# Row-tiled paired transposes, a softmax without row max, and shared PSUM banks in a two-block attention kernel

## Chip, cores and metric

One core of a Trainium2 chip. The metric is the device time of one execution in microseconds (us); smaller is better. "PE" is the matmul engine (its weight loads are a row of their own, "PEld"), DVE the vector engine, ACT the activation engine, POOL the general engine, SP the engine that issues the loads. All runs quoted here were classed as fast, and PE's granted clock is given where it matters.

## The reference

Two independent attention blocks A and B, with their outputs side by side. In each there are 16 batch entries, 64 queries, 32 heads, 512 cached keys and a head size of 128, all bf16:

```python
q = (x @ wq).reshape(B, Sq, H, Dh).transpose(0, 2, 1, 3)      # x: 16 x 64 x 640
scores = einsum("bhqd,bhkd->bhqk", q, k_cache) * Dh ** -0.5
p = softmax(scores)
o = einsum("bhqk,bhkd->bhqd", p, v_cache)
out = o.transpose(0, 2, 1, 3).reshape(B, Sq, H * Dh) @ wo      # 16 x 64 x 640
# result: concatenate([out_A, out_B], -1)
```

The caches make up 268 MB of the 295 MB that the core reads, and nothing of them is used twice.

## The kernel before

The kernel is a static software pipeline. Its unit, called a step here, is two heads of two batch entries; there are 256 steps, fully unrolled. Every engine runs its own straight-line list of instructions, and semaphores tie the lists together. K and P are transposed on PE, because in this kernel's matmuls the index that is summed over lies on the partitions of both operands. One `transpose` or `matmul` in this code becomes two PE instructions, a weight load and a matmul.

```python
# PE's order in one step; the numbers are offsets in steps
PE_T = (("TR2", 1), ("QP2", 4), ("KX", 4, 0), ("SM2", 3), ("PV2", 1), ("XT", 0), ("OP2", 0), ("KX", 4, 1))
# ...
def em_KX(e, op):                       # K: 8 transposes of 128x128, twice a step
    # ...
    for t8 in range(8):
        ins = e.transpose(kt_ps[:, t8, :], kn_ring[:, c % NKB, j, hp, t8, :], ident[:, :])
# ...
def em_MX(e, op):                       # row max, on DVE
    ins = e.reduce_max(negmax[:, r:r + 1], s_bank(g % 2), axis=AX.X, negate=True)

def em_EX(e, op):                       # exp and row sum, on ACT
    ins = e.activation(p_ring[:, g % NP, :], s_bank(g % 2), ACTF.Exp, bias=negmax[:, r:r + 1], scale=1.0,
                       accum_out=rowsum[:, r:r + 1])
# ...
def em_TR2(e, op):                      # P: 8 transposes of 128x128 a step
    # ...
    for t in range(4):
        ins = e.transpose(pt_ps[:, sub, t, :], pn_ring[:, g % NPN, t * 128:(t + 1) * 128], ident[:, :])
```

K and V come in loads of 512 KB into rings of five chunks (10 MB together), all issued by SP as soon as a chunk's place is free.

Of the kernel before, what the change touches and what calls it, by code (L numbers as in the profile page):

```python
# [5 lines left out]
BF16 = mybir.dt.bfloat16  # L6
F32 = mybir.dt.float32
ACTF = mybir.ActivationFunctionType
# [3 lines left out]
ENGINES = ("sp", "pe", "act", "dve", "pool")  # L12


class Cfg:
# [4 lines left out]
    NX = 2  # L20
    NXN = 1
    XLEAD = 10
    NQ = 2
    NKT = 2
    NP = 4
    NPN = 3
    NT = 2
    NO = 2
    NR = 8
    PE_T = (("TR2", 1), ("QP2", 4), ("KX", 4, 0), ("SM2", 3), ("PV2", 1), ("XT", 0), ("OP2", 0), ("KX", 4, 1))  # L30
    ACT_T = (("QE2", 4), ("OE2", 1), ("XE", 0), ("EX", 3, 0), ("EX", 3, 1), ("OV", 0), ("ST", -1))
    DVE_T = (("TE2", 1), ("RC2", 2), ("KE", 4, 0), ("MX", 3, 0), ("MX", 3, 1), ("KE", 4, 1), ("OVF", 0))
    POOL_T = (("NM", 0, 0), ("NM", 0, 1))
    TAIL_SPLIT = 2
    SLOT_NS = 3600.0
    DMA_NS = dict(LDK=3100.0, LDV=3100.0, LDWQ=3900.0, LDWO=4300.0, LDX=700.0)


class Op:
# [3 lines left out]
    def __init__(self, eng, kind, idx, reads=(), writes=(), dur=0.0, ts=None, aux=None):  # L43
        self.eng = eng
        self.kind = kind
        self.idx = idx
        self.reads = tuple(reads)
        self.writes = tuple(writes)
        self.sem = None
        self.count = None  # L50
        self.deps = []
        self.waits = []
        self.dur = dur
        self.ts = ts
        self.aux = aux
        self.dma = kind in ("LDK", "LDV", "LDX", "LDWQ", "LDWO", "ST")


STAGES = ("LDW", "LDX", "LDK", "LDV", "KX0", "KE0", "KX1", "KE1", "QP2", "QE2", "SM2", "MX0", "MX1", "EX0", "EX1",
          "RC2", "NM0", "NM1", "TR2", "TE2", "XT", "XE", "PV2", "OE2", "OP2", "OV", "ST")  # L60
STAGE_IDX = {s: i for i, s in enumerate(STAGES)}
SUB_KINDS = ("KX", "KE", "EX", "NM", "MX")


def build_plan(dims, cfg):
# [7 lines left out]
    SPB = HH  # L73
    NPASS = NBLK * NHALF
    NSTEP = NPASS * NBP * SPB
    NMAC = NSTEP // 2
    NCHUNK = NSTEP // G
    NGRP = NPASS * NBP
    HG = HH // G
    MPG = SPB // 2  # L80
    MPP = NBP * MPG
    MPC = G // 2
    KT = dims["KT"]

    def step_info(g):
        grp = g // SPB
        return grp // NBP, grp % NBP, grp, g % SPB

    progs = {e: [] for e in ENGINES}

    def mk(eng, kind, idx, reads, writes, stage, m_ts, sub=0, aux=None, dur=0.0):
        return Op(eng, kind, idx, reads, writes, dur=dur, aux=aux, ts=(m_ts, STAGE_IDX[stage], sub))

    OFF = {}
    for t in cfg.PE_T:
        OFF.setdefault(t[0], t[1])

    def make_op(kind, m, sub):
        g0, g1 = 2 * m, 2 * m + 1
        ps_, bp, grp, h0 = step_info(g0)  # L100
        c = g0 // G
        if kind == "KX":
            return mk("pe", "KX", (m, sub), [("kn", c % cfg.NKB, g0 % G), ("kn", c % cfg.NKB, g1 % G), ("ident",)],
                      [("KTB",)], "KX%d" % sub, m, sub)
        if kind == "KE":
            return mk("dve", "KE", (m, sub), [], [("KTB",), ("ktp", m % cfg.NKT, sub)], "KE%d" % sub, m, sub)
        if kind in ("MX", "EX", "NM"):
            g = 2 * m + sub
            r = g % cfg.NR
            if kind == "MX":  # L110
                return mk("dve", "MX", g, [], [("SB", sub), ("negmax", r)], "MX%d" % sub, m, sub)
            if kind == "EX":
                return mk("act", "EX", g, [("negmax", r)], [("SB", sub), ("p", g % cfg.NP), ("rowsum", r)],
                          "EX%d" % sub, m, sub)
            return mk("pool", "NM", g, [("p", g % cfg.NP), ("recip", r)], [("pn", g % cfg.NPN)], "NM%d" % sub, m, sub)
        r0, r1 = g0 % cfg.NR, g1 % cfg.NR
        if kind in ("XT", "XE"):
            mt = m + cfg.XLEAD
            if mt % MPG != 0 or not (0 <= mt < NMAC):
                return None  # L120
            gq = mt // MPG
            m_ts = mt - cfg.XLEAD + OFF["TR2"]
            if kind == "XT":
                return mk("pe", "XT", gq, [("xn", gq % cfg.NXN), ("ident",)], [("PTB",)], "XT", m_ts, aux=gq)
            return mk("act", "XE", gq, [], [("PTB",), ("xT", gq % cfg.NX)], "XE", m_ts, aux=gq)
        if kind == "QP2":
            return mk("pe", "QP2", m, [("xT", grp % cfg.NX), ("wq", ps_ % 2, h0 // G)], [("QB",)], "QP2", m)
        if kind == "QE2":
            return mk("act", "QE2", m, [], [("QB",), ("qT", m % cfg.NQ)], "QE2", m)
        if kind == "SM2":  # L130
            return mk("pe", "SM2", m, [("qT", m % cfg.NQ), ("ktp", m % cfg.NKT, 0), ("ktp", m % cfg.NKT, 1)],
                      [("SB", 0), ("SB", 1)], "SM2", m)
        if kind == "RC2":
            return mk("dve", "RC2", m, [("rowsum", r0), ("rowsum", r1)], [("recip", r0), ("recip", r1)], "RC2", m)
        if kind == "TR2":
            return mk("pe", "TR2", m, [("pn", g0 % cfg.NPN), ("pn", g1 % cfg.NPN), ("ident",)], [("PTB",)], "TR2", m)
        if kind == "TE2":
            return mk("dve", "TE2", m, [], [("PTB",), ("pT", m % cfg.NT)], "TE2", m)
        if kind == "PV2":
            return mk("pe", "PV2", m, [("pT", m % cfg.NT), ("v", c % cfg.NVB, g0 % G), ("v", c % cfg.NVB, g1 % G)],  # L140
                      [("OB",)], "PV2", m)
        if kind == "OE2":
            return mk("act", "OE2", m, [], [("OB",), ("oT", m % cfg.NO)], "OE2", m)
        if kind == "OP2":
            return mk("pe", "OP2", m, [("oT", m % cfg.NO), ("wo", ps_ % 2, h0 // G)], [("OUTB",)], "OP2", m)
        if kind in ("OV", "OVF", "ST"):
            if h0 + 1 != SPB - 1:
                return None
            last_half = ps_ % NHALF == NHALF - 1
            if kind == "OV":  # L150
                if NHALF == 1:
                    return mk("act", "OV", m, [], [("OUTB",), ("out_sb", grp % 2)], "OV", m, aux=grp)
                if last_half:
                    return None
                return mk("act", "OVP", m, [], [("OUTB",), ("outp", bp)], "OV", m, aux=grp)
            if kind == "OVF":
                if NHALF == 1 or not last_half:
                    return None
                return mk("dve", "OVF", m, [("outp", bp)], [("OUTB",), ("out_sb", grp % 2)], "OV", m, aux=grp)
            if NHALF == 1 or not last_half:  # L160
                return None
            return mk("act", "ST", m, [("out_sb", grp % 2)], [("out_dram", grp)], "ST", m, aux=grp)
        raise ValueError(kind)

    templates = {"pe": cfg.PE_T, "dve": cfg.DVE_T, "pool": cfg.POOL_T, "act": cfg.ACT_T}
    for eng, tmpl in templates.items():
        offs = [t[1] for t in tmpl] + [cfg.XLEAD]
        for k in range(-max(offs), NMAC - min(offs)):
            for t in tmpl:
                kind, off = t[0], t[1]  # L170
                sub = t[2] if len(t) > 2 else 0
                if kind in ("XT", "XE"):
                    op = make_op(kind, k, 0)
                    if op is not None:
                        progs[eng].append(op)
                    continue
                m = k + off
                if 0 <= m < NMAC:
                    op = make_op(kind, m, sub)
                    if op is not None:  # L180
                        progs[eng].append(op)
                        if op.kind == "OV":
                            progs[eng].append(mk("act", "ST", m, [("out_sb", op.aux % 2)], [("out_dram", op.aux)],
                                                 "ST", m, aux=op.aux))

    progs["pool"] = [mk("pool", "INIT1", -1, [], [("ones",)], "LDW", -10),
                     mk("pool", "INIT2", -1, [("ones",)], [("ident",)], "LDX", -10)] + progs["pool"]
# [3 lines left out]
    for ps_ in range(NPASS):  # L191
        first_m = ps_ * MPP
        buf = ps_ % 2
        for j in range(HG):
            m0 = first_m + j * MPC
            if ps_ < 2:
                rq = ro = NEG
            else:
                last_use = (ps_ - 1) * MPP - MPG + j * MPC + MPC - 1
                rq = last_use - OFF["QP2"]  # L200
                ro = last_use - OFF["OP2"]
# [518 lines left out]
```

## Time and profile before

| | before |
|---|---|
| time, median of 3 | 958.91 us (958.47 to 959.11) |
| PE, DVE, ACT, POOL busy | 96%, 88%, 59%, 44% |
| one step in the steady state | 3.57 us |
| data rate, mean | 313 GB/s |

The engine line, the two rows of clock and data rate over 40 equal slices, two lines of the DMA queues (packets, MB, share of the 16 DMA engines) and the chain that ended last, from the page of the kernel before:

```profile
PE 919.4 (96%) x14755; PEld 733.5 (77%) x15008; DVE 841.9 (88%) x1552; ACT 567.1 (59%) x1585; POOL 416.9 (44%) x518
...
PEclk9999999999999999999999999999999999999999
...
GB/s 315 364 365 364 351 365 367 365 368 351 338 337 337 343 330 315 299 292 305 322 332 352 326 353 327 306 294 296 302 305 288 308 301 297 295 297 314 295 124 15
...
q1 hardware_dynamic: 228416, 294.69, 91.0%
q8 instruction: 118, 1.93, 0.8%
...
PE 89%; DVE 4%; POOL 3%; issue 2%; SPq 1%; DMA 1%; POOLq 0%; DVEq 0%
```

PE is busy throughout and owns the chain, so PE sets the time. Queue q1 brings the data; in q8, 118 packets bring the instructions themselves. 1.93 MB in 118 packets is 16 KB a packet; the count of records below shows that one holds 256 of PE's instructions.

The timeline of PE over one step of the kernel before (start, length, engine, line, what it writes and reads, shapes, count; a group that runs long overlaps the next, so steps are read from start to start):

```profile
500.75 0.61 PE L433 MATMUL ps<-ident,kn_ring 128*128 128x128 bf16 x8
501.19 0.61 PE L505 MATMUL ps<-ident,pn_ring 128*128 128x128 bf16 x8
501.64 0.72 PE L451 MATMUL ps<-xT_ring,wq_sb 128*128 128x128 bf16 x10
502.20 0.61 PE L433 MATMUL ps<-ident,kn_ring 128*128 128x128 bf16 x8
502.74 0.62 PE L467 MATMUL ps<-ktp_ring,qT_ring 128*64 128x512 bf16 x4
503.30 0.64 PE L524 MATMUL ps<-pT_ring,v_ring 128*128 128x64 bf16 x16
...
504.31 0.28 PE L433 MATMUL ps<-ident,kn_ring 128*128 128x128 bf16 x2
```

From 500.75 to 504.31 there is no gap. The transposes (lines 433 and 505) take 24 x 55.6 ns = 1.33 us of the 3.57.

### The profile page before, as it was taken

The page shows a single profiled execution, that of the slowest core. Times are in us where ns is not written, and L with a number is a line of the kernel's source. Part 1 is how long each engine was busy: PE and PEld are TensorE (multiplying, and loading weights), DVE is VectorE, ACT ScalarE, POOL GpSimd, SP SyncE. Part 2 cuts the span into 40 slices and gives each one's busy share as a digit, 9 for nine tenths or more (in the row PEclk, how much of TensorE's full clock was granted, in tenths as well). Part 3 has the DMA queues.
Part 4 walks back from the last instruction along what each step waited for, and adds up shares of the span by engine and source line. Part 5 has one row for each costly group of instructions (what it writes and reads, how often), then busy time and mean ns, then how long its engine had stood idle before and what let it go on. Part 6 is the DMA issues. An engine that isn't in the chain of part 4 may idle for free.

```text
span 956.8 us, 34351 instructions
## 1 busy us (share of the span) xinstructions
PE 919.4 (96%) x14755; PEld 733.5 (77%) x15008; DVE 841.9 (88%) x1552; ACT 567.1 (59%) x1585; POOL 416.9 (44%) x518
## 2 busy tenths in 40 slices
PE   4999999999999999999999999999999999999997
PEld 3877777778777777877777787777877778777775
DVE  2898899898899999899999899889899998999996
ACT  1666656666665565656566666666666656565654
POOL 0444444444444444444444444444444444444443
PEclk9999999999999999999999999999999999999999
DMA  9999999999999999888999999988888988899830
GB/s 315 364 365 364 351 365 367 365 368 351 338 337 337 343 330 315 299 292 305 322 332 352 326 353 327 306 294 296 302 305 288 308 301 297 295 297 314 295 124 15
DMA packets 230871, 299.51 MB, mean 313 GB/s; under 512 B 9536, under 2 KB 165184, under 8 KB 230720
## 3 DMA queue, kind: packets, MB, share of 16 engines
q1 hardware_dynamic: 228416, 294.69, 91.0%
q8 instruction: 118, 1.93, 0.8%
q10 hardware_dynamic: 2304, 2.62, 0.8%
q14 instruction: 33, 0.27, 0.1%
HBM read 294.65 MB, written 2.62 MB: 311 GB/s over the span
## 4 chain that ended last, share of the span: by engine, by line
PE 89%; DVE 4%; POOL 3%; issue 2%; SPq 1%; DMA 1%; POOLq 0%; DVEq 0%
PE ps L433 22%; PE ps L524 14%; PE ps L451 14%; PE ps L467 14%; PE ps L505 12%; PE ps L545 7%; PE ps L540 5%; POOL pn_ring L496 3%; DVE out_sb L560 1%; DVE ktp_ring L442 1%; DVE pT_ring L512 1%; PE ps L604 1%; DMA xn_ring<-in_A_x_dram 1%; SPq L626 1%; SPq L583 1%
## 5 line engine op out<-in xcount | busy, mean ns | idle before, releaser
L496 POOL TENSOR_SCALAR pn_ring<-p_ring,recip 128x512 bf16<-128x512 bf16 x512 | 416.3, 843 | 532.7 <-DVE recip L488 532.7
L442 DVE COPY ktp_ring<-ps 128x1024 bf16<-128x1024 bf16 x512 | 353.7, 691 | 105.3 <-PE ps L433 85.1
L482 ACT ACTIVATE p_ring<-ps,negmax 128x512 bf16<-128x512 f32 x512 | 345.6, 684 | 4.8 <-DVE negmax L476 4.8
L476 DVE TENSOR_REDUCE negmax<-ps 128x1 f32<-128x512 f32 x512 | 327.3, 681 | 0.4 <-PE ps L467 0.3
L433 PE MATMUL ps<-ident,kn_ring 128*128 128x128 bf16 x4096 | 314.6, 220 | 2.8 <-DMA kn_ring<-in_A_k_cache_dram 1.6
L532 ACT ACTIVATE oT_ring<-ps 128x256 bf16<-128x256 f32 x256 | 98.0, 383 | 306.0 <-PE ps L524 306.0
L433 PEld LDWEIGHTS ps<-ident,kn_ring 128*128 128x128 bf16 x4096 | 251.9, 98 | 34.2 <-DVE ktp_ring L442 2.6
L524 PEld LDWEIGHTS ps<-pT_ring,v_ring 128*128 128x128 bf16 x4096 | 133.5, 98 | 109.2 <-issue 100.0
L451 PE MATMUL ps<-xT_ring,wq_sb 128*128 128x128 bf16 x2560 | 186.4, 220 | 3.2 <-DMA wq_sb<-in_A_wq_dram 3.2
L512 DVE COPY pT_ring<-ps 128x1024 bf16<-128x1024 bf16 x256 | 174.5, 682 | 4.6 <-PE ps L505 3.8
L524 PE MATMUL ps<-pT_ring,v_ring 128*128 128x64 bf16 x4096 | 163.8, 194 | 3.3 <-issue 1.7
L467 PE MATMUL ps<-ktp_ring,qT_ring 128*64 128x512 bf16 x1024 | 159.8, 392 | 0.4 <-ACT p_ring L482 0.4
L505 PE MATMUL ps<-ident,pn_ring 128*128 128x128 bf16 x2048 | 156.7, 219 | 3.5 <-POOL pn_ring L496 3.5
L451 PEld LDWEIGHTS ps<-xT_ring,wq_sb 128*128 128x128 bf16 x2560 | 155.2, 98 | 3.5 <-DMA wq_sb<-in_A_wq_dram 3.5
L459 ACT ACTIVATE qT_ring<-ps 128x256 bf16<-128x256 f32 x256 | 98.4, 384 | 66.8 <-PE ps L451 66.8
L505 PEld LDWEIGHTS ps<-ident,pn_ring 128*128 128x128 bf16 x2048 | 124.1, 98 | 7.0 <-POOL pn_ring L496 6.7
L545 PE MATMUL ps<-wo_sb,oT_ring 128*128 128x128 bf16 x512 | 112.1, 219 | 13.4
L482 ACT ACTIVATION_READ_ACCUMULATOR p_ring<-ps,negmax 128x1 f32 x512 | 105.0, 205 | 0.0
L540 PE MATMUL ps<-wo_sb,oT_ring 128*128 128x512 bf16 x259 | 97.8, 379 | 0.0
L540 PEld LDWEIGHTS ps<-wo_sb,oT_ring 128*128 128x128 bf16 x512 | 50.1, 98 | 30.6 <-ACT oT_ring L532 0.3
L467 PEld LDWEIGHTS ps<-ktp_ring,qT_ring 128*64 128x64 bf16 x1024 | 36.1, 108 | 27.1 <-ACT p_ring L482 0.6
L545 PEld LDWEIGHTS ps<-wo_sb,oT_ring 128*128 128x128 bf16 x512 | 50.1, 98 | 0.0
(13 smaller groups left out, 112.7 us busy)
## 6 DMA issues: line engine op xcount, KB each, us to landing
kn_ring<-in_A_k_cache_dram SPq DMA_DIRECT2D x128, 512.0 KB, 7.0
v_ring<-in_A_v_cache_dram SPq DMA_DIRECT2D x128, 512.0 KB, 7.2
kn_ring<-in_B_k_cache_dram SPq DMA_DIRECT2D x126, 512.0 KB, 4.8
v_ring<-in_B_v_cache_dram SPq DMA_DIRECT2D x126, 512.0 KB, 5.7
wq_sb<-in_A_wq_dram SPq DMA_DIRECT2D x8, 640.0 KB, 10.4
wo_sb<-in_A_wo_dram SPq DMA_DIRECT2D x8, 640.0 KB, 10.2
wq_sb<-in_B_wq_dram SPq DMA_DIRECT2D x8, 640.0 KB, 8.4
wo_sb<-in_B_wo_dram SPq DMA_DIRECT2D x8, 640.0 KB, 7.5
```

The costliest lines, as they stand in the source:

```text
L433: ins = e.transpose(kt_ps[:, t8, :], kn_ring[:, c % NKB, j, hp, t8, :], ident[:, :])
L442: ins = e.tensor_copy(dst, src)
L451: ins = e.matmul(q_ps[:, sub * 128:(sub + 1) * 128], wq_sb[:, ps_ % 2, kt, hh * DH:(hh + 1) * DH], xT_ring[:, grp % NX, kt, :], start=(kt ...
L467: ins = e.matmul(s_bank(sub)[64 * j:64 * j + 64, :], qT_ring[:, m % NQ, sub, 64 * j:64 * j + 64], ktp_ring[:, m % NKT, sub, j, :], start=T ...
L476: ins = e.reduce_max(negmax[:, r:r + 1], s_bank(g % 2), axis=AX.X, negate=True)
L482: ins = e.activation(p_ring[:, g % NP, :], s_bank(g % 2), ACTF.Exp, bias=negmax[:, r:r + 1], scale=1.0, accum_out=rowsum[:, r:r + 1])
L496: ins = e.tensor_scalar(dst, src, recip[:, r:r + 1], 1.0, ALU.mult, ALU.mult)
L505: ins = e.transpose(pt_ps[:, sub, t, :], pn_ring[:, g % NPN, t * 128:(t + 1) * 128], ident[:, :])
L512: ins = e.tensor_copy(pT_ring[:, m % NT].rearrange("p s t q -> p (s t q)"), pt_ps_flat)
L524: ins = e.matmul(o_ps[:, col:col + 64], v_ring[:, c % NVB, j, gi, t, :], pT_ring[:, m % NT, sub, t, 64 * j:64 * j + 64], start=(t == 0), s ...
L540: ins = e.matmul(out_ps0, oT_ring[:, m % NO, sub, :], wo_sb[:, ps_ % 2, hh, 0:N0], start=(hh == 0), stop=(hh == SPB - 1))
L545: last = e.matmul(out_ps1, oT_ring[:, m % NO, sub, :], wo_sb[:, ps_ % 2, hh, N0:DN], start=(hh == 0), stop=(hh == SPB - 1))
```

## The change

The intent was to take work from PE and DVE.

1. Each 128x128 transpose becomes two transposes of 64 rows on the two row halves of the array ("row-tiled"), issued as pairs that may run at once.
2. The row max goes. The exponential is taken of the scaled scores directly, all row sums are kept, and after the last step a check on the chip decides whether a second, general program with the row max has to run.
3. The P and Q evictions are rearranged: Q's goes from ACT to DVE, P's is cut in two.
4. Two PSUM banks are shared by P transposes, Q and P·V: PE fills both, then DVE and ACT drain them.

The core of the diff (cut; the plan, the load order and the final branch are left out):

```diff
-    PE_T = (("TR2", 1), ("QP2", 4), ("KX", 4, 0), ("SM2", 3), ("PV2", 1), ("XT", 0), ("OP2", 0), ("KX", 4, 1))
+    ENGINE_ORDER = dict(
+        pe=("KX0", "TR0", "QP0", "PV0", "XT0", "OP0", "SM0", "SM1"),
 ...
+        def row_transpose(e, dst, src, r):
+            return e.transpose(dst, src, ident[rows(r), rows(r)], tile_position=(64 * r, 0))
 ...
-            for t8 in range(8):
-                ins = e.transpose(kt_ps[:, t8, :], kn_ring[:, c % NKB, j, hp, t8, :], ident[:, :])
+            for j in range(2):
+                for t8 in range(8):
+                    for hs in PAIR:
+                        col = 512 * j + 64 * t8
+                        ins.append(row_transpose(e, kt_ps(hs)[:, col:col + 64],
+                                                 kn_ring[rows(hs), c % NKB, j, hp, t8, :], hs))
 ...
+                kw = dict(bias=bias[:, r:r + 1]) if stable else {}
+                ins = e.activation(p_ring[:, g % NP, :], ps[:, S_BANK + g % 2, :], ACTF.Exp, scale=scale,
+                                   accum_out=sums[:, g:g + 1], **kw)
 ...
                 for t in range(4):
-                    ins = e.transpose(pt_ps[:, sub, t, :], pn_ring[:, g % NPN, t * 128:(t + 1) * 128], ident[:, :])
+                    for j in PAIR:
+                        ins.append(row_transpose(e, pt_ps(j)[:, sub, t, :],
+                                                 pn_ring[rows(j), g % NPN, t * 128:(t + 1) * 128], j))
```

24 transposes a step become 48.

## The prediction

> **What bounds it now.** The matmul engine (PE): the engine table gives it 919.4 of 956.8 us (96%), DVE 88%, ACT 59%; the chain of waits is 89% PE. The timeline around 500 us repeats one step (two heads, two batch entries; 256 steps) every 3.57 us without a PE gap. Start to start: K transposes 0.88, P transposes 0.45, Q projection 0.56, scores 0.43, P·V 0.47, output projection 0.54, about 0.1 us on each side of the column-tiled scores. 256 x 3.565 = 912.6 us; some 44 us are start and tail.
> The second limit is close: the stretches from 10 to 200 us move 361 to 366 GB/s with the DMA share over 1; later 300 to 340. 294.7 MB at 365 GB/s is an estimated 807 us, 3.15 us a step.
>
> **What changes.**
> 1. Each transpose becomes two 64-row ones on different row tiles, 24 pairs a step. P·V, also 64 columns with a weight load each, runs at 29 ns a matmul; the 128-column transposes at 55.6. If a pair runs at once, 24 x 29 ns = 0.70 us replaces 1.33. The Trainium skill, "TensorE: Matmul & The Clock Gate", Part 3, says that matmuls of different row tiles start about 4 ns apart; nothing in this trace shows row tiles. Without overlap, 48 x 29 = 1.40 us: no gain.
> 2. One more change of tiling mode per step (three). The skill, "TensorEngine Tiling (Array Packing)", Key Properties, says a change drains the array; this trace shows 0.10 to 0.13 us beside the scores. Estimate +0.1 us.
>    PE step: 0.70 + 2.00 + 0.35 = 3.05 us; 256 x 3.05 + 44 = 825 us.
> 3. The row max leaves DVE (2 x 0.60 us start to start). The Q eviction comes to DVE (estimate 0.33), the P eviction splits in two (0.33 each), the reciprocal in two. DVE falls from about 3.3 to 2.4 us a step, below PE. ACT loses the Q eviction (0.38). Neither bounded, so alone this is worth little.
> 4. P transposes, Q and P·V fill two shared banks that DVE and ACT drain before the next P transposes. DVE should finish 0.3 us before that: no large PE wait.
> 5. Check, flag and branch: a few us, once; no rerun.
>
> **What remains.** PE at 3.05 us asks for more than DMA gives (3.15), so I expect DMA to bind for much of the run: 807 + about 5 to start + 10 for the tail, and some loss as two nearly equal limits interleave.
>
> **Prediction: 832 us, 8 in 10 between 812 and 875.** Faster by over 2%: 0.93; within 2%: 0.04; slower: 0.03.
>
> **What would show it right or wrong.**
> - Step 1: K and P transposes near 0.70 us a step, pairs 29 ns apart; wrong near 1.3.
> - Step 2: three gaps of about 0.1 us beside tiled groups.
> - Step 3: DVE busy 650 to 700 us; no row-max group.
> - Step 4: wrong if PE waits for DVE or ACT by over 0.1 us a step.
> - DMA: near 365 GB/s for nearly the whole span; PE waits for loads of K, V or weights.
> - Rerun: no second pass.
>
> **What would make it wrong.** Row tiles that run one after another (890 to 1000 us); bank sharing that puts DVE into each step's chain (860 to 880); a DMA rate not held at 365, or one above it (down to 810).

## The result, and the profile after

The changed kernel takes 1028.11 us (median of 4, 1023.66 to 1035.58) against 959.01 us for the kernel before (median of 4). The ratio is 1.073, with a 95% interval of 1.069 to 1.077: slower, where a gain of 13% was forecast. Ratios here are the mean time of one kernel's fast runs over that of the other's fast runs of the same rounds, so not quite the ratio of the quoted medians. The profiled execution took 1035.58 us, the longest of the four.

The lines of the changed kernel's page that answer to those above:

```profile
PE 837.1 (81%) x20900; PEld 606.1 (59%) x21153; DVE 669.2 (65%) x1812; ACT 447.8 (43%) x1329; POOL 416.9 (40%) x518
...
PEclk9899999999998999999999999999989999989998
...
GB/s 317 365 366 348 279 312 297 304 303 309 272 296 288 299 321 302 314 271 314 345 282 300 221 278 344 303 300 271 269 320 366 290 247 280 264 290 327 292 146 12
...
q1 hardware_dynamic: 228416, 294.69, 84.4%
q8 instruction: 170, 2.79, 1.1%
...
PE 77%; issue 16%; DVE 4%; SPq 1%; DMA 1%; ACT 1%; ACTq 0%; DVEq 0%
```

PE's busy time did fall, by 82 us. But no engine is above 81% now, and the data rate fell as well, so neither an engine nor the data is the limit. What grew is "issue" in the chain, from 2% to 16%: time in which PE waited for no semaphore, yet did not run. The instruction packets grew from 118 to 170.

The waits of the changed kernel (who, for whom: us in total, times, longest):

```profile
PEld ps L431 <- issue: 175.7, 282, 3.1
...
PE ps L431 <- issue: 73.4, 53, 2.9
...
PE ps L535 <- issue: 36.5, 24, 2.3
...
PE ps L457 <- issue: 27.0, 14, 2.9
...
PE ps L551 <- issue: 8.8, 22, 2.0
```

These waits stand before every kind of PE work (K and P transposes are L431, P·V L535, Q L457, the output L551), each up to 2 or 3 us. Loads of K and V are hardly named as a cause. A PE timeline of the changed kernel shows one such wait in the middle of a group, where no semaphore could stand:

```profile
505.10 0.55 PE L431 MATMUL ps<-ident,kn_ring 64*128 64x64 bf16 x26
507.14 0.26 PE L431 MATMUL ps<-ident,kn_ring 64*128 64x64 bf16 x6 [1.49 <-issue]
507.26 0.41 PE L431 MATMUL ps<-ident,pn_ring 64*128 64x64 bf16 x16
```

The 32 transposes of one K group are cut after 26. Counting the records of PE's instructions gave the pattern: 93 of the 103 places where PE started nothing for over 0.6 us lie on a grid of 254.5 records (the other ten lie in the first 23 and the last 18 us). The grid is 256 instructions less the few that the trace lost (253 matmuls in all), which is one instruction packet.

The packets' own times close the loop. Around this stall PE resumes at 500.30 us from the stall before; the next instruction packet starts at 504.53 and ends at 505.61; PE starts its last instruction at 505.46, and resumes at 507.14. Over all stalls the medians are 4.0 us from a resume to the start of the next packet, 1.06 us for the packet, and 1.42 us from its end to PE's resume (middle half 1.35 to 1.50, all 91 stalls of the table below between 1.2 and 1.7). The last figure is so steady that the packet's arrival is what PE waits for. One block of 256 instructions then takes some 6.5 us, an estimate by the sum of these medians; a quarter of the waits from a resume to the next packet were under 2.0 us. The kernel before used a block up in 256 / 117.5 x 3.57 = 7.8 us and never ran dry. The changed one wants a block every 256 / 167.3 x 3.04 = 4.7 us.

### The profile page after: what moved, and what is told of

Its sections match the earlier page's. It is cut to its first block, busy times and chain, and to the rows that moved or that the text cites. A ratio compares the mean times of both kernels' runs of the same rounds, so it can differ in the third digit from the quotient of the medians.

```text
span 1033.8 us, 47133 instructions
## 1 busy us (share of the span) xinstructions
PE 837.1 (81%) x20900; PEld 606.1 (59%) x21153; DVE 669.2 (65%) x1812; ACT 447.8 (43%) x1329; POOL 416.9 (40%) x518
## 4 chain that ended last, share of the span: by engine, by line
PE 77%; issue 16%; DVE 4%; SPq 1%; DMA 1%; ACT 1%; ACTq 0%; DVEq 0%
PE ps L431 21%; PE ps L457 16%; PE ps L470 14%; PE ps L551 12%; PE ps L535 12%; DVE ktp_ring L447 2%; PE ps L631 1%; DMA xn_ring<-in_A_x_dram 1%; DVE pT_ring L522 1%; ACT p_ring L491 1%; DVE out_sb L564 0%; SPq L646 0%; SPq L650 0%; SPq L611 0%; DVE qT_ring L463 0%
## 5 line engine op out<-in xcount | busy, mean ns | idle before, releaser
L491 ACT ACTIVATE p_ring<-ps 128x512 bf16<-128x512 f32 x512 | 301.1, 594 | 53.4 <-PE ps L470 24.0
L522 DVE COPY pT_ring<-ps 128x512 bf16<-128x512 bf16 x512 | 193.1, 419 | 129.3 <-PE ps L535 128.8
L431 PEld LDWEIGHTS ps<-ident,kn_ring 64*128 64x128 bf16 x8192 | 141.5, 97 | 147.0 <-issue 131.7
L457 PE MATMUL ps<-xT_ring,wq_sb 128*128 128x128 bf16 x2560 | 198.3, 226 | 31.0 <-issue 27.0
L535 PE MATMUL ps<-pT_ring,v_ring 128*128 128x64 bf16 x4096 | 174.2, 197 | 36.5 <-issue 36.5
L431 PE MATMUL ps<-ident,kn_ring 64*128 64x64 bf16 x8192 | 175.8, 194 | 32.8 <-issue 30.7
L535 PEld LDWEIGHTS ps<-pT_ring,v_ring 128*128 128x128 bf16 x4096 | 153.6, 101 | 42.2 <-issue 41.6
L457 PEld LDWEIGHTS ps<-xT_ring,wq_sb 128*128 128x128 bf16 x2560 | 150.7, 100 | 45.4 <-issue 27.8
L551 PE MATMUL ps<-wo_sb,oT_ring 128*128 128x128 bf16 (+1 forms) x771 | 134.1, 285 | 21.2 <-issue 8.8
L431 PE MATMUL ps<-ident,pn_ring 64*128 64x64 bf16 x4096 | 108.9, 192 | 47.0 <-issue 42.6
L463 DVE CAST qT_ring<-ps 128x256 bf16<-128x256 f32 x256 | 108.5, 424 | 17.8 <-PE ps L457 9.2
L431 PEld LDWEIGHTS ps<-ident,pn_ring 64*128 64x128 bf16 x4096 | 81.7, 96 | 48.4 <-issue 44.1
L491 ACT ACTIVATION_READ_ACCUMULATOR p_ring<-ps 128x1 f32 x512 | 102.4, 200 | 0.0
L551 PEld LDWEIGHTS ps<-wo_sb,oT_ring 128*128 128x128 bf16 x1024 | 76.1, 101 | 39.8 <-issue 12.0
L498 DVE RECIPROCAL recip<-sums 128x1 f32<-128x1 f32 x512 | 78.5, 153 | 8.1 <-ACT p_ring L491 8.1
```

The costliest lines, as they stand in the source:

```text
L431: return e.transpose(dst, src, ident[rows(r), rows(r)], tile_position=(64 * r, 0))
L457: ins.append(e.matmul(q_ps[:, sub * 128:(sub + 1) * 128], wq_sb[:, ps_ % 2, kt, hh * DH:(hh + 1) * DH], xT_ring[:, grp % NX, kt, :], start ...
L463: ins = e.tensor_copy(qT_ring[:, op.idx % NQ].rearrange("p s q -> p (s q)"), q_ps)
L491: ins = e.activation(p_ring[:, g % NP, :], ps[:, S_BANK + g % 2, :], ACTF.Exp, scale=scale, accum_out=sums[:, g:g + 1], **kw)
L498: ins = e.reciprocal(recip[:, g % NR:g % NR + 1], sums[:, g:g + 1])
L522: ins = e.tensor_copy(pT_ring[:, m % NT, j].rearrange("p s t q -> p (s t q)"), ps[:, A_BANK + j, 0:256].bitcast(BF16))
```

## The experiments

The theory, F (fetch): PE's program streams in by packets of 256 instructions on the same DMA engines as the data; the packet stands behind K and V data; row tiling raised the instructions per us of PE work until PE runs dry. The rivals: P, that the shared PSUM banks or the new order make PE wait for DVE and ACT; R, that row tiling costs time by itself when the loads run at full rate.

The count of PE stalls below leaves out the first 50 and the last 40 us of each profiled run. A stall is over 0.6 us from one PE start to the next. The last column counts those stalls that end 1.2 to 1.7 us after the end of an instruction packet, as all 91 of the change do: these are waits for instructions. The others are mostly waits for K and V loads by name.

| run | PE instructions a step (recorded) | median us | stalls, us in all | of these, after a packet |
|---|---|---|---|---|
| before | 117 | 959 | 0, 0 | 0 |
| the change | 167 | 1028 | 91, 161 | 91 |
| e1 the change, light loads | 167 | 851 | 6, 8 | 6 |
| e2 no tiling | 117 | 957 | 0, 0 | 0 |
| e6 P tiled | 134 | 959 | 1, 1 | 1 |
| e5 K tiled | 152 | 969 | 67, 82 | 67 |
| e7 the change, smaller pieces | 168 | 989 | 109, 140 | 70 |
| e8 the change, 1 MB in flight | 168 | 1063 | 122, 204 | 25 |
| e11 the change, 1.5 MB in flight | 168 | 965 | 84, 116 | 84 |
| e9 K tiled in every second step | 133 | 926 | 6, 6 | 6 |
| e10 K tiled, 1.5 MB in flight | 151 | 919 | 27, 34 | 10 |
| e12 both tiled in every second step, 1.5 MB | 143 | 921 | 13, 19 | 1 |

### e1: light loads

```diff
             if op.kind == "LDV":
+                if c >= NVB:
+                    src, hhi = src[:, 0:1], hlo + 1
                 ins = e.dma_start(v_ring[:, c % NVB, j, hlo:hhi], src)
 ...
+                if c >= NKB:
+                    ins = e.dma_start(kn_ring[:, c % NKB, j, hlo // 2, 0:4], src[:, 0, 0:4])
+                else:
                     ins = e.dma_start(kn_ring[:, c % NKB, j, hlo // 2:hhi // 2], src)
```

> The changed kernel with every K and V load after the first five chunks cut to a quarter of its bytes (wrong results on purpose; the same instructions on every engine). Theory F, instruction fetch: the trace of the changed kernel shows PE idle for 1 to 3 us every 255 records, ending 1.4 us after a 16 KB packet of the instruction queue; that packet starts about 4 us after PE last resumed, because it stands behind K and V data. With light loads that wait shrinks, a block comes well within the 4.8 us that PE takes to use one up, the stalls vanish, and the step becomes PE-bound at 3.05 to 3.25 us: 825 to 875 us in all. Theory P, shared PSUM banks: PE waits for DVE and ACT, which are untouched: still 990 to 1030 us.

Measured: 850.96 us, wrong results as intended (ratio to before 0.888). From the page of e1, the engines and the queues, then one step of its PE timeline:

```profile
PE 790.7 (93%) x20900; PEld 579.7 (68%) x21153; DVE 665.1 (78%) x1812; ACT 445.6 (53%) x1329; POOL 416.8 (49%) x518
...
q1 hardware_dynamic: 102976, 101.75, 39.2%
q8 instruction: 170, 2.79, 1.4%
```

```profile
501.02 0.64 PE L431 MATMUL ps<-ident,kn_ring 64*128 64x64 bf16 x32
501.50 0.40 PE L431 MATMUL ps<-ident,pn_ring 64*128 64x64 bf16 x16
501.83 0.73 PE L457 MATMUL ps<-xT_ring,wq_sb 128*128 128x128 bf16 x10
502.40 0.63 PE L535 MATMUL ps<-pT_ring,v_ring 128*128 128x64 bf16 x16
503.08 0.49 PE L551 MATMUL ps<-wo_sb,oT_ring 128*128 128x128 bf16 x3
503.50 0.62 PE L470 MATMUL ps<-ktp_ring,qT_ring 128*64 128x512 bf16 x4
504.06 0.32 PE L431 MATMUL ps<-ident,kn_ring 64*128 64x64 bf16 x10
```

PE executes the same instructions in the same order, and the step takes 3.04 us (501.02 to 504.06). Theory P falls: banks, order, DVE and ACT are unchanged and PE does not wait for them. Taking away data removed 153 us of the 161 us of stalls. The same block boundaries of the same PE program can be compared in both runs: from a boundary to the start of the next instruction packet the median is 3.7 us with full loads and 0.9 us with light ones. This run alone does not tell whether it was the instructions' wait or K and V's own lateness that went; the next ones do.

### e2: no tiling

```diff
-                    for hs in PAIR:
-                        col = 512 * j + 64 * t8
-                        ins.append(row_transpose(e, kt_ps(hs)[:, col:col + 64], kn_ring[rows(hs), c % NKB, j, hp, t8, :], hs))
+                    ins.append(e.transpose(kt_ps(j)[:, 128 * t8:128 * t8 + 128], kn_ring[:, c % NKB, j, hp, t8, :], ident[:, :]))
 ...  (the same for P; the two evictions take the other layout)
```

> The changed kernel with all transposes as in the kernel before, 128 columns wide and not row-tiled; all else of the change kept: no row max, Q eviction on DVE, banks shared by phase, check, flag, branch, second program. PE's stream falls from 167 to about 118 instructions a step. Theory F: a block lasts 7.7 us, longer than a refill, so no stalls, and PE needs its old 3.57 us a step: 950 to 965 us. Theory P: the shared banks and the order are still there, so it stays above 1000 us.

Measured: 957.06 us, correct, ratio 0.998 (0.996 to 1.000). All else of the change is in it, with DVE at 679 us busy and ACT at 446, and it is worth 0.2%. So the row max, the moved evictions, the shared banks, the check, the branch and the second program, taken together, neither cost nor gain; the run does not part them. The whole loss comes with the tiled transposes. The K transposes of e2, then its P transposes, and the start of what follows them:

```profile
500.99 1.07 PE L439 MATMUL ps<-ident,kn_ring 128*128 128x128 bf16 x16
501.90 0.61 PE L515 MATMUL ps<-ident,pn_ring 128*128 128x128 bf16 x8
502.34 0.72 PE L457 MATMUL ps<-xT_ring,wq_sb 128*128 128x128 bf16 x10
```

### e3 and e4: extra instructions in the kernel before

```diff
+        def idle(e):
+            e.wait_ge(sems[("s_init",)], 1)
+            e.wait_ge(sems[("d_x", 0)], 16)
 ...  (between two transposes or matmuls of a group)
+                if t8:
+                    idle(e)
```

> The kernel before with 44 more sequencer instructions a step in PE's stream: waits for semaphores that are long satisfied; no other work changes. The stream grows from 118 to 162 instructions a step. Theory F: at 3.57 us a step a block lasts 5.6 us, less than the 6.5 us of a refill under load, so stalls of about 1 us at most block ends: 1000 to 1070 us, with PE idle every 256 instructions. Theory P, or a cost of row tiling itself: nothing here has changed, 955 to 975 us.

> Control for the one with extra waits: the same extra instructions, with K and V loads after the first five chunks cut to a quarter (wrong results on purpose). Theory F: blocks come in time, so the extra instructions by themselves cost little: 945 to 975 us. If the waits themselves slow PE down, it stays as long as the run without light loads, and that run proves nothing about the fetch.

Measured: 1569.39 us with full loads and 1566.37 us with light ones. This pair was a failure of design. The control rules out the conclusion that the first run seems to invite: each inserted pair of long-satisfied waits, one recorded instruction more, costs PE some 54 ns by itself ((1569 - 959) us / (44 x 256)), so the kernel became bound by the waits and used its blocks up slowly. Nothing about the fetch follows. So no run here raised the instruction count without tiling; that it is the count which does the harm is argued from the packets' times and from the runs below.

### e5 and e6: tiling one of the two

> The changed kernel with the P transposes undone (full 128-column ones), the K transposes row-tiled: 152 PE instructions a step. PE alone would need an estimated 3.04 + 0.22 = 3.26 us a step (light-load run plus the P transposes' difference), so a block lasts 5.5 us, a little less than the 6.0 us median block time seen under full load. Theory F: stalls remain but are shorter, 925 to 985 us. Rival R, that row tiling itself costs time under full load (its weight loads, its mode changes): the excess over the version without tiling goes with the tiled transposes, 32 of 48, so about 1004 us.

> The changed kernel with the K transposes undone, only the P transposes row-tiled: 134 PE instructions a step. PE alone needs an estimated 3.04 + 0.43 = 3.47 us a step, so a block lasts 6.6 us, about what a refill takes. Theory F: nearly no stalls, 930 to 955 us, faster than both the kernel before and the one without tiling. Rival R: 16 of 48 tiled, about 981 us.

The edits are one half each of the diff of e2. Measured: K alone 969.10 us, ratio 1.012 (1.007 to 1.016); P alone 959.33 us, ratio 1.001 (0.999 to 1.003). Theory R wanted about 1004 and 981. The excess does not go with the number of tiled transposes: P's 16 cost 2 us over e2, K's 32 cost 12, all 48 cost 71. It goes with the stalls, which begin between 134 and 152 instructions a step.

For P alone the estimate of 930 to 955 us missed, and the timeline of e6 shows why:

```profile
502.76 1.07 PE L439 MATMUL ps<-ident,kn_ring 128*128 128x128 bf16 x16
503.76 0.41 PE L431 MATMUL ps<-ident,pn_ring 64*128 64x64 bf16 x16
504.10 0.73 PE L457 MATMUL ps<-xT_ring,wq_sb 128*128 128x128 bf16 x10
...
506.32 0.28 PE L439 MATMUL ps<-ident,kn_ring 128*128 128x128 bf16 x2
```

The step is 3.56 us, as long as without tiling. The P group shrank to 0.34 us (0.44 in e2), but the K group before it now takes 1.00 us up to the next start (0.91 in e2), which fits a change of the tiling mode between them. A group of 16 just pays for its own change of mode.

### e7: smaller pieces

```diff
-                ins = e.dma_start(v_ring[:, c % NVB, j, hlo:hhi], src)
+                for t in (0, 2):
+                    ins.append(e.dma_start(v_ring[:, c % NVB, j, hlo:hhi, t:t + 2], src[:, :, t:t + 2]))
 ...  (K likewise in two halves of four)
```

> The changed kernel with each K and V load cut in two, so that the contiguous pieces are 1 KB for K and 512 bytes for V (2 KB and 1 KB before); the same bytes, the same PE instructions. If an instruction packet stands behind a fixed number of data pieces, its wait (3.7 us median from a block's end to the start of the next packet) falls to about 2 us and the time to 900 to 980 us. If it stands behind a fixed amount of bytes, nothing changes: 1010 to 1040 us. If small pieces lower the data rate below 300 GB/s, PE waits for K and V and it is slower still.

Measured: 988.92 us, ratio to before 1.033, so 4% faster than the change, and between the ranges for pieces and for bytes, but for a mixed reason. The wait from a block's end to the next packet fell from 3.7 to 2.8 us (medians). The data rate was flat at 289 to 328 GB/s up to the tail, with the DMA engines over 90% busy, and PE now also waited for K loads by name. It moved from one limit to another, and what exactly an instruction packet stands behind (pieces or bytes) stays open.

### e8 and e11: fewer bytes in flight

```diff
-        n = cfg.TAIL_SPLIT if c == NCHUNK - 1 else 1
+        n = cfg.TAIL_SPLIT                            # all loads in halves: 256 KB
 ...
+                if op.eng == "sp":
+                    pair = op.kind in ("LDK", "LDV")
+                    if len(flying) >= 2 and not (pair and op.aux[1] == 1):      # 3 in e10, e11 and e12
+                        s, v = flying.pop(0)
+                        e.wait_ge(sems[s], v * step(s))
+                    if not pair or op.aux[1] == 1:
+                        flying.append((op.sem, op.count))
```

> The changed kernel with at most two pairs of 256 KB K or V loads (1 MB) in flight, the queue holding back the next until the one before last has landed; the same bytes, piece sizes and PE instructions. Theory F: fewer bytes ahead of an instruction packet, its wait falls below 2.9 us (1 MB at 365 GB/s), and the time to 930 to 1000 us, unless the data rate falls so much that PE waits for K and V loads by name, which would show in the waits. Theory P or R: no change, about 1028 us.

> The changed kernel whole (all transposes row-tiled, 168 PE instructions a step), only the loads held to three pairs of 256 KB (1.5 MB) in flight. Theory F: an instruction packet waits less than with the queue full and more than with 1 MB in flight (medians 3.7 and 2.1 us), say 2.9 us, so a block takes about 5.4 us, still over the 4.6 us that PE needs at 3.04 us a step: stalls shrink but stay, 168 x 5.4 + 40 = 950 us, 930 to 985 us. Theory P or R: no change, about 1028 us.

With 1 MB in flight: 1063.39 us, slower. It took the branch that the expectation named: the instruction packets did wait less (about 2.0 us by block boundaries), but the data rate sank to about 290 GB/s and PE waited for K. Two lines of its waits:

```profile
PEld ps L431 <- DMA kn_ring<-in_B_k_cache_dram: 95.8, 62, 3.7
...
PEld ps L431 <- DMA kn_ring<-in_A_k_cache_dram: 82.3, 57, 3.0
```

With 1.5 MB in flight: 964.59 us, ratio 1.004. This is the changed kernel with every matmul, eviction, bank and byte in place; only the loads differ, cut in halves of 256 KB and held back in the queue, and this took 64 us off it. (Halves without the cap were not run.) After a stall the next instruction packet now starts 2.8 us later instead of 4.0 (medians), and the stalls fell from 161 to 116 us. By block boundaries the median wait is 2.8 us, so it falls with what is in flight: 3.7 us without a cap, 2.8 with 1.5 MB, 2.0 with 1 MB, 0.9 with light loads. (This trace lost no matmul records, and neither did those of e7 and e8: a block is 256 records there, not 254.5.)

### e9, e10 and e12: between the two limits

If F is right, the best version is neither of the two kernels: tile only as much as the packets can feed, or feed faster. e9 tiles K in every second step, P not at all:

```diff
                 for t8 in range(8):
+                    if m % 2:
+                        ins.append(e.transpose(kt_ps(j)[:, 128 * t8:128 * t8 + 128],
+                                               kn_ring[:, c % NKB, j, hp, t8, :], ident[:, :]))
+                        continue
                     for hs in PAIR:
```

e10 is e5 with 1.5 MB in flight. e12 tiles K and P in every second step, with 1.5 MB in flight.

> The changed kernel with full P transposes, and the K transposes row-tiled in every second step only: 134 PE instructions a step on average, 152 and 118 by turns. PE alone needs an estimated (3.26 + 3.56) / 2 = 3.41 us a step, so a block of 256 lasts 6.5 us, a little longer than the 6.0 us median block time under load. Theory F: few and short stalls, 256 x 3.41 + 48 = 921 us plus some stalls: 915 to 950 us, faster than the kernel before and than every version with more or less tiling. Rival R, a cost of tiling under load: between the version without tiling (957) and the one with K tiled in all steps (969), so 957 to 970 us.

> K transposes row-tiled in all steps, P transposes full (152 PE instructions a step), with at most three pairs of 256 KB loads (1.5 MB) in flight. Theory F: the wait of an instruction packet falls from a median of 4.1 us to about 3 us, a block comes in about 5.5 us, which is what PE uses up in 5.5 us at 3.26 us a step; the data rate should hold 340 GB/s with 1.5 MB in flight. 900 to 960 us, against 969 us without the cap. If the data rate stays at 300 GB/s as with 1 MB in flight, PE waits for K loads by name and it is slower than 969 us.

> All transposes (K and P) row-tiled in every second step, full in the others: 143 PE instructions a step on average, and 1.5 MB of loads in flight. PE alone needs (3.04 + 3.56) / 2 = 3.30 us a step, a block lasts 5.9 us and comes in about 5.4. Theory F: hardly any stalls, 256 x 3.30 + 55 = 900 us; the data rate of 335 to 345 GB/s seen with 1.5 MB in flight sets a floor of 295 MB / 340 = 866 us plus start and tail. 890 to 925 us, at or below the best so far (919).

Measured: e9 926.43 us, ratio 0.967 (0.965 to 0.969); e10 919.46 us, 0.961 (0.958 to 0.964); e12 920.77 us, 0.961 (0.959 to 0.963). All correct, all in their ranges, and all faster than both kernels. e9 is the sharpest test of R: it lies between e2 (957) and e5 (969) in its tiling, and outside them in its time. A cost in proportion to the tiling cannot do that; a threshold on instructions per us can. e6 and e9 have the same instruction count, and neither stalls for more than 6 us in all; e9 gains because a tiled K group pays for its mode change and more: in its timeline the steps with tiled K take 3.24 us and the others 3.57, K going from 0.90 us to 0.57 up to the next start:

```profile
502.30 1.07 PE L440 MATMUL ps<-ident,kn_ring 128*128 128x128 bf16 x16
503.20 0.61 PE L525 MATMUL ps<-ident,pn_ring 128*128 128x128 bf16 x8
...
505.87 0.64 PE L431 MATMUL ps<-ident,kn_ring 64*128 64x64 bf16 x32
506.44 0.62 PE L525 MATMUL ps<-ident,pn_ring 128*128 128x128 bf16 x8
...
509.11 1.07 PE L440 MATMUL ps<-ident,kn_ring 128*128 128x128 bf16 x16
```

The engine line of e10, its data rate, and two lines of its waits:

```profile
PE 843.3 (92%) x18852; PEld 632.6 (69%) x19105; DVE 678.1 (74%) x1812; ACT 446.7 (49%) x1329; POOL 419.0 (46%) x518
...
GB/s 266 310 338 335 335 327 343 330 338 337 331 338 342 322 320 340 335 346 350 353 354 333 329 337 324 335 341 342 358 335 323 357 336 340 351 329 347 347 326 13
...
PEld ps L431 <- DMA kn_ring<-in_B_k_cache_dram: 17.0, 16, 2.9
...
PEld ps L431 <- DMA kn_ring<-in_A_k_cache_dram: 10.6, 15, 2.1
```

The rate is now near 340 GB/s for most of the span: 295 MB at 340 GB/s is 867 us, so e10 and e12 have come close to the data as their next limit. Their stalls say the same: in e10 only 10 of 27 (9 us of 34) follow an instruction packet, in e12 only 1 of 13, and all but three of the others are waits for K, V or weight loads by name. This may be why a further fall in instructions (e12) brought nothing more; no run tested it.

## Why the prediction was wrong

- **Step 1, pairs: right.** K and P pairs ran at once. In e1, 32 K transposes take 0.48 us from start to start and 16 P ones 0.33, a change of mode included; the two of a pair mostly start 3 or 4 ns apart and the pairs 29, both as foreseen.
- **Step 2, modes: right.** "PE step: 0.70 + 2.00 + 0.35 = 3.05 us" was 3.04 us in e1, where nothing starved PE. e6 shows a further change of mode at about 0.09 us.
- **Step 3, DVE and ACT: right.** DVE fell to 669 us (650 to 700 foreseen). e2 shows that without the tiling all this is worth 0.2%.
- **Step 4, shared banks: right.** PE does not wait for DVE or ACT in e1 and e2.
- **Step 5, check and branch: right.** e2 carries them at no loss; no second pass ran.
- **"What remains" was the step that failed:** "so I expect DMA to bind for much of the run: 807 + about 5 to start + 10 for the tail". The rate after was 291 GB/s on the mean, lower than before (313), and PE's waits hardly name a load. The list of limits, PE at 3.05 us and data at 3.15 us a step, lacked a third: the supply of PE's own instructions. It is 256 instructions per 6.5 us under full loads, 25 ns an instruction, so 167 x 25 ns = 4.2 us a step if every packet came that late. The measured step was (1028 - 44) / 256 = 3.84 us, since not every packet did. A tiled pair adds two instructions (50 ns of supply) to save 26 ns of array time. Where supply is the limit, that is a loss. The data term was too low besides: no run with full loads held 365 GB/s; the best means were 327 (e10, e12) and 324 (e9), and the best time 919 us, so the fetch is not all of what parts 1028 from 832 us.
- The numbers were on the page beforehand: 118 packets of 16 KB in 957 us is one in 8.1 us, and 167 instructions in 3.05 us asks for one in 4.7 us. What the trace before could not show is how long a packet takes when asked for sooner, because PE never ran dry there. If the block boundaries lie there as in the change, its packets start a median of some 2.2 us after a boundary, which with 1.1 and 1.4 us makes an estimated 4.7 us a block: no clear warning. The Trainium skill, "Runtime: NRT & Kernel Launch", section "Instruction fetch mechanics", does describe the stream of blocks of 256 instructions, fetched on a DMA queue of the engine's own. It calls the cost of crossing a block "mostly hidden". This trace agrees with the block size and, for the changed kernel, not with the hiding: 91 stalls and 161 us.

Not settled: of the 186 us between the profiled runs of the change and of e1 (spans 1033.8 and 848.2), 153 are stalls over 0.6 us. The rest includes shorter stalls and the lower granted clock (0.952 against 0.991). Stalls alone did not lower it: e5, with 67 of 1.2 us on the mean, kept 0.997, where the change's 91 took 1.8 us each. These runs do not split the rest. Also open is whether a packet waits behind pieces, bytes or both, and why it waits longer in the change (3.7 us) than in the kernel before (some 2.2 us) and in e2 (2.7 us), whose loads are the same.

## What to carry to other kernels

Count an engine's instructions per us of its work as a limit beside its busy time and the data rate: an edit that replaces one instruction by two half-size ones may double the demand on instruction supply even when the array time halves. In a profile the sign is "issue" idle time in the middle of a group, evenly spaced by instruction count. Heavy loads lengthened the wait for instructions here (3.7 us against 0.9 in e1), so try tiling only a part, and try fewer bytes in flight, before giving the faster instruction up; here the two together turned a loss of 7% into a gain of 4%.

## What the Trainium skill lacked or had wrong

- "Runtime: NRT & Kernel Launch", "Instruction fetch mechanics": it says that the fetch is mostly hidden, since the sequencer dispatches slower than blocks come. With PE at 167 instructions in 3 us and data near 300 GB/s it was not: 4.0 us from a resume to the start of the next packet, 1.06 us for the packet, 1.42 us until PE resumed; 91 stalls, 161 us. The page gives 2,048 instructions of instruction memory for PE and, lower down, two lines of 16 KiB; in 52 of 90 cases PE ran dry one packet (256 instructions) after it had last resumed, in the others after two to four.
- "DMA: Bandwidth & Descriptors": nothing on instruction packets that share the engines with data. Halving the loads and holding them to 1.5 MB in flight still allowed about 340 GB/s (e10) and took 64 us off the changed kernel (e11); at 1 MB the rate fell to about 290 GB/s.
- "TensorE: Matmul & The Clock Gate", "Back-to-back issue gap": it gives a floor of about 25 ns for matmuls of up to 64 columns. 32 row-tiled transposes of 64 columns on two row tiles, each with its own weight load, took 0.48 us, 15 ns each, because two start together: each row tile by itself kept 29 ns, as did P·V, 64 columns without row tiles. The floor is not contradicted; the section does not say that it holds for each row tile apart.
- "TensorEngine Tiling (Array Packing)", "Key Properties": a change of mode drains the array, but no figure is given. Here some 0.09 us (e6, beside P) to 0.13 us (kernel before, beside the scores) go with one.
- No page was found with the cost of long-satisfied semaphore waits in PE's stream, only with the time that a sequencer takes to read a semaphore's value: about 54 ns for an inserted pair of waits (e3).
